# The first loads of a fused attention and feed-forward kernel: alpha and k of chunk 0 ahead of the first weight slice

## The chip, the cores and the metric

The kernel runs on one core of one Trainium2 chip. The metric is device time in microseconds (us), lower is better. The kernel before takes 539.71 us (median of three runs, 539.61 to 539.85).

## The reference

A gated recurrence over 768 tokens is computed for 4 batches and 8 heads of width 48. Its output, turned to 3072 rows of 384, goes through a feed-forward block with a hard-swish:

```python
for t in range(S):
    state = alpha[:, :, t, :, None] * state + einsum('bhd,bhe->bhde', k[:, :, t], v[:, :, t])
    y[:, :, t] = einsum('bhd,bhde->bhe', q[:, :, t], state)
x = y.transpose(0, 2, 1, 3).reshape(B * S, H * D)      # 3072 x 384
h = x @ w_in                                           # 384 x 2048
g = h * clip(h + 3, 0, 6) / 6
out = g @ w_out                                        # 2048 x 384
```

q, k, v and alpha are float32. w_in and w_out are float64; the chip gets their bits as pairs of 32-bit words.

## The kernel before

**Attention by chunks.** The tokens are cut into 24 chunks of 128 (six to a batch). Products of alpha over time are made with scans along the free axis, so alpha, k and q of a chunk are turned on TensorE first. For the first six chunks these inputs are loaded straight, 192 KB each and in pieces of 192 bytes, into a ring of three places.

**Weights by slices.** The two weight matrices arrive in 16 slices of 768 KB. Each float64 is decoded to a float32 by integer and float steps on ACT, DVE and GpSimd (POOL). Raw slices share five buffers, so later slices wait for the decoding of earlier ones.

**Feed-forward by groups.** Two chunks make a group of 256 tokens. The first groups use plain products; from group 1 or 2 on the two matrix products use sums of blocks, so that fewer block products are needed.

**The order.** There is no scheduler: one long list of words, read once from left to right, emits every instruction. Each word is a step with its chunk, slice or group and at times a PSUM bank. Each engine, and the Sync queue (SP) which issues all loads and stores, runs its own instructions in exactly that order; semaphores join the engines. Moving a word changes its place only in the queues that its instructions go to.

The words that the change and the prediction use:

| word | what it does | engine, lines |
|---|---|---|
| z.m.n | n idle 128x128 products of the identity into bank m, read by nobody | TensorE, L532, two instructions each |
| la.j, lk.j, lq.j | load alpha, k, q of chunk j | SP, L251 |
| lv.j | load v of chunk j in two halves | SP, L272 |
| w.i | load weight slice i | SP, L162 (w_in), L166 (w_out) |
| ta.j, tk.j, tq.j | turn alpha, k, q of chunk j | TensorE, L282 |
| ca.j | copy the turned alpha out of PSUM | ACT, L300 |
| r.j | scan of alpha from the chunk's end, and a reciprocal | DVE, L309, L313 |
| k.j, q.j | scale k by r.j, and q by p.j | DVE, L332 |
| p.j | scan of alpha from the chunk's start | DVE, L320 |
| d2.i | magnitude of slice i's high words (an activation with Abs) | ACT, L196 |
| d1.i | slice i's low words rounded (an activation with Copy) | ACT, L186 |
| dx.i | slice i's signs | ACT, L191 |
| d3.i | clamp and shift of slice i's high words | DVE, L203 and L205, or L207, L208 and L210 |
| d4.i | high and low words added | POOL, L217 |
| kb.j, ck.j | k.j turned back to rows by token, and copied out of PSUM | TensorE L374, ACT L378 |
| u.j | update of the state from k and v, two halves | TensorE, L429 |
| sm.j.b | new state after half b of chunk j | DVE, L437 (chunk 0, half 0), L439 |
| sv.j.b | state placed beside v (for chunk 0, half 0: zeros) | ACT, L419 (POOL, L415) |
| sc.j, m.j | scores within a chunk, and their mask | TensorE L346, DVE L356 |

qa.0.0 emits nothing, since chunk 0 starts a batch. The activations of d2 and d1 are `nc.scalar.activation(...)`; the copies of ca and ck are `nc.scalar.copy(...)`, which the profile shows as COPY and not as ACTIVATE. In program order the first instruction of ACT is d2.0, ahead of ca.0.

At the head of the list the Sync queue holds w.0, la.0, lk.0, la.1, lq.0, lk.1, lv.0 (two halves), la.2, w.2 and so on. TensorE holds 17 idle products, ta.0, tk.0, two idle products, ta.1, tq.0, kb.0, two idle products, u.0.

Of the kernel before, what the change touches and what calls it, by code (L numbers as in the profile page):

```python
# [17 lines left out]
def kernel(  # L18
# [553 lines left out]
    for i in range(8):  # L572
        r, o = divmod(i, 3)
# [175 lines left out]
    def run(words):  # L749
        for word in words.split():  # L750
            name, *at = word.split(".")
            steps[name](*(int(x) for x in at))

    with tc.manual_schedule():
        run("""z.0.5 z.0.3 z.0.1 z.0.8 qa.0.0 w.0 d2.0 d3.0 la.0 ta.0.0 ca.0 r.0 lk.0 tk.0.1 k.0
               z.0.2 p.0 la.1 ta.1.2 lq.0 tq.0.3 ca.1 r.1 lk.1 lv.0.0 sv.0.0 d1.0 kb.0.0 ck.0 z.0.2
               u.0.2.1 sm.0.0 sv.0.1 q.0 qa.0.1 tk.1.0 k.1 p.1 z.0.2 sc.0.2.3 m.0 la.2 ta.2.0 ca.2
               dx.0 w.2 d2.2 kb.1.0 ck.1 lq.1 r.2 sm.0.1 st.1 tq.1.2 q.1 d3.2 z.0.3 d1.2 dx.2
               lv.1.1 u.1.3.1 sv.1.0 sm.1.0 p.2 sm.1.1 sc.1.0.2 m.1 ya.0.3 yb.0 cy.0 lq.2 w.1 d1.1
# [179 lines left out]
```

## Time and profile before

| | |
|---|---|
| runs | 539.71, 539.85, 539.61 us |
| profiled execution: span from first to last instruction | 538.1 us |
| between the span and the median of the runs | 1.6 us |
| busy share of the span: TensorE, DVE, ACT, POOL | 98%, 88%, 48%, 9% |
| DMA: moved in the span, mean rate | 54.40 MB, 101 GB/s |
| granted TensorE clock | 1.000 |

The profile gives the span of the profiled execution; what lies around it is taken as the difference to the median of the runs, 1.6 us. In the views times are microseconds from the span's start. A row in order of time has start, duration, engine, line, operation, what is written and read with shapes and count, and in brackets the engine's idle time just before with what ended it. A row of waits has who waited, for whom, the total, how often, and the longest. The DMA view gives, for an issue, the time from issue to landing.

### The profile page before, as it was taken

How to read it: one execution, taken by the hardware profiler on the slowest of the kernel's cores; microseconds unless marked ns; L12 is line 12 of the kernel's file. 1: busy time of each engine (PE TensorE's matmuls, PEld its weight loads, DVE VectorE, ACT ScalarE, POOL GpSimd, SP SyncE). 2: the span in 40 equal slices, each digit the busy share in tenths (PEclk: the TensorE clock that was granted, in tenths of full speed). 3: DMA queues.
4: the chain of work that ended last, by engine and by line, in shares of the span. 5: the costliest groups of instructions: out<-in, count | busy, mean ns of one | idle time of the engine just before them, and what ended most of it. 6: DMA issues, size and time to landing. Idle time of an engine off the chain costs nothing.

```text
span 538.1 us, 15166 instructions
## 1 busy us (share of the span) xinstructions
PE 526.3 (98%) x6306; PEld 499.7 (93%) x6306; DVE 475.3 (88%) x839; ACT 259.6 (48%) x513; POOL 50.4 (9%) x71
## 2 busy tenths in 40 slices
PE   8799999999999999999999999999999999999997
PEld 7688886789999999999999999999999999999996
DVE  6999989999999899989999898999999898495481
ACT  3889865212653553543544444642644544553230
POOL 5333425100000000000010000000000000000000
PEclk9999999999999999999999999999999999999999
DMA  9998876006625156263444355155354042100001
GB/s 172 211 251 250 218 217 154 17 2 154 149 35 117 30 117 141 46 140 86 94 109 112 89 121 137 21 127 120 88 136 103 15 103 42 44 3 1 15 16 37
DMA packets 124101, 54.40 MB, mean 101 GB/s; under 512 B 83329, under 2 KB 116865, under 8 KB 124033
## 3 DMA queue, kind: packets, MB, share of 16 engines
q1 hardware_dynamic: 124032, 53.44, 43.7%
q8 instruction: 49, 0.80, 0.7%
q14 instruction: 20, 0.16, 0.1%
HBM read 44.50 MB, written 8.91 MB: 99 GB/s over the span
## 4 chain that ended last, share of the span: by engine, by line
PE 83%; DVE 10%; DMA 3%; ACT 1%; issue 1%; SPq 0%; POOL 0%; DVEq 0%; ACTq 0%; POOLq 0%
PE m_ps L703 32%; PE m_ps L600 32%; PE m_ps L478 6%; PE t_ps L455 4%; PE t_ps L346 2%; PE t_ps L429 2%; DMA v<-in_v_dram 2%; PE m_ps L532 1%; PE m_ps L489 1%; PE m_ps L516 1%; DVE rings L647 1%; DVE R L309 1%; DVE raw L537 1%; DVE g_sb L647 1%; DVE w L537 1%
## 5 line engine op out<-in xcount | busy, mean ns | idle before, releaser
L703 PE MATMUL m_ps<-w,g_sb 128*128 128x192 f32 x704 | 122.1, 327 | 0.6 <-ACT m_ps L709 0.5
L606 ACT COPY g_sb<-m_ps 128x512 f32<-128x512 f32 x110 | 63.5, 584 | 114.7 <-PE m_ps L600 98.2
L703 PEld LDWEIGHTS m_ps<-w,g_sb 128*128 128x128 f32 x704 | 113.7, 190 | 1.7 <-ACT m_ps L709 0.8
L703 PE MATMUL m_ps<-rings,g_sb 128*128 128x192 f32 x528 | 91.6, 327 | 0.6 <-ACT u L682 0.6
L703 PEld LDWEIGHTS m_ps<-rings,g_sb 128*128 128x128 f32 x528 | 85.3, 190 | 1.0 <-ACT u L682 0.9
L600 PE MATMUL m_ps<-xc,w 128*128 128x128 f32 x640 | 82.7, 277 | 0.2 <-DVE w L541 0.2
L600 PEld LDWEIGHTS m_ps<-xc,w 128*128 128x128 f32 x640 | 77.5, 192 | 1.4 <-issue 0.4
L494 ACT ACTIVATE r<-g_sb,half 128x512 f32<-128x512 f32 x80 | 56.7, 722 | 29.4 <-DVE g_sb L541 11.7
L498 DVE SCALAR_TENSOR_TENSOR g_sb<-r,g_sb 128x512 f32<-128x512 f32 x80 | 53.6, 682 | 7.5 <-ACT r L494 7.0
L600 PE MATMUL m_ps<-xT,raw 128*128 128x128 f32 x400 | 52.6, 278 | 0.9 <-ACT g_sb L606 0.9
L600 PEld LDWEIGHTS m_ps<-xT,raw 128*128 128x128 f32 x400 | 48.6, 192 | 1.9 <-ACT g_sb L606 1.2
L409 POOL TENSOR_TENSOR st<-sm,R 128x192 f32<-128x192 f32 x20 | 12.9, 643 | 355.8 <-DVE sm L439 306.7
L647 DVE TENSOR_TENSOR g_sb<-g_sb 128x512 f32<-128x512 f32 (+1 forms) x55 | 42.0, 792 | 1.4 <-PE m_ps L703 1.1
L600 PE MATMUL m_ps<-xT,w 128*128 128x128 f32 x320 | 42.0, 276 | 0.0
L600 PEld LDWEIGHTS m_ps<-xT,w 128*128 128x128 f32 x320 | 39.3, 192 | 0.1
L366 ACT COPY A<-q 48x256 f32<-48x256 f32 x88 | 35.6, 404 | 4.9 <-DVE q L332 3.7
L356 DVE TENSOR_TENSOR A<-t_ps,mask 64x256 f32<-64x256 f32 x96 | 36.1, 414 | 0.4
L478 PE MATMUL m_ps<-xT,w 128*128 128x256 f32 x144 | 32.8, 382 | 0.0
L600 PE MATMUL m_ps<-xc,raw 128*128 128x128 f32 x240 | 31.8, 276 | 0.0
L309 DVE TENSOR_TENSOR_SCAN R<-t,ones 128x516 f32<-128x516 f32 x24 | 29.5, 1231 | 1.3 <-ACT t L300 1.2
L478 PEld LDWEIGHTS m_ps<-xT,w 128*128 128x128 f32 x144 | 26.7, 190 | 3.6
L600 PEld LDWEIGHTS m_ps<-xc,raw 128*128 128x128 f32 x240 | 29.6, 192 | 0.1
(105 smaller groups left out, 730.0 us busy)
## 6 DMA issues: line engine op xcount, KB each, us to landing
raw<-in_moe_w_out_dram SPq DMA_DIRECT2D x8, 768.0 KB, 4.8
raw<-in_moe_w_in_dram SPq DMA_DIRECT2D x6, 768.0 KB, 7.0
v<-in_v_dram SPq DMA_DIRECT2D x48, 96.0 KB, 3.2
out_dram<-oh SPq DMA_DIRECT2D x44, 96.0 KB, 1.8
far<-kq SPq DMA_DIRECT2D x64, 64.0 KB, 2.2
kb<-far SPq DMA_DIRECT2D x64, 64.0 KB, 2.0
aq<-in_alpha_dram SPq DMA_DIRECT2D x36, 96.0 KB, 2.6
qq<-in_q_dram SPq DMA_DIRECT2D x36, 96.0 KB, 2.5
```

The costliest lines, as they stand in the source:

```text
L309: nc.vector.tensor_tensor_scan(out=reverse(R, n - 1, n), data0=reverse(ax, n, n), data1=reverse(ones, n, n), initial=0.0, op0=ALU.mult, op ...
L356: nc.vector.tensor_tensor(out=to[:, a], in0=sc[a][half], in1=mask[half, half].unsqueeze(1).to_broadcast([HB, NP, HB]), op=ALU.mult)
L366: nc.scalar.copy(out=to[:, a], in_=Q_t[j][64 * a : 64 * a + D, :, half])
L409: nc.gpsimd.tensor_tensor(out=st, in0=sm, in1=R_t[j][:, :, 0:1].to_broadcast([C, NP, D]), op=ALU.mult)
L455: nc.tensor.matmul(y_of(j, (i + 1) // 2, p)[:, HB * b : HB * b + HB], vb[:, p, e : e + 32], A_t[j][:, b, 2 * p + a], start=(b == 0 and i = ...
L478: nc.tensor.matmul(h[:, f], w1[:, kk, o : o + C], xT_t[g][:, kk], start=(kk == 0), stop=(kk == KT - 1))
L494: nc.scalar.activation(out=to, in_=h, func=AF.Relu, bias=half, scale=1.0 / 6.0)
L498: nc.vector.scalar_tensor_tensor(out=to, in0=r, scalar=1.0, in1=h, op0=ALU.min, op1=ALU.mult)
L600: nc.tensor.matmul(acc[g][i][:, f * C : (f + 1) * C], spots[w][:, f * C : (f + 1) * C], x_of(g, x), start=(first and f == 0), stop=last, s ...
L606: nc.scalar.copy(out=slots[z], in_=acc[g][i])
L647: nc.vector.tensor_tensor(out=out, in0=in0, in1=in1, op=ALU.subtract)
L703: nc.tensor.matmul(to[g], a, rhs[:, f], start=(first and f == 0), stop=(last and f == HF - 1), skip_group_check=True)
```

## The change

The head of the list is reordered. The words from w.0 to lk.0 and the decoding steps d2.0 and d3.0 change places, and the idle products at the start change in number.

```diff
-        run("""z.0.5 z.0.3 z.0.1 z.0.8 qa.0.0 w.0 d2.0 d3.0 la.0 ta.0.0 ca.0 r.0 lk.0 tk.0.1 k.0
-               z.0.2 p.0 la.1 ta.1.2 lq.0 tq.0.3 ca.1 r.1 lk.1 lv.0.0 sv.0.0 d1.0 kb.0.0 ck.0 z.0.2
+        run("""z.0.5 z.0.3 qa.0.0 la.0 lk.0 w.0 la.1 ta.0.0 ca.0 r.0 tk.0.1 k.0 z.0.6
+               p.0 ta.1.2 lq.0 ca.1 r.1 d2.0 tq.0.3 lk.1 lv.0.0 sv.0.0 d3.0 d1.0 kb.0.0 ck.0 z.0.2
                u.0.2.1 sm.0.0 sv.0.1 q.0 qa.0.1 tk.1.0 k.1 p.1 z.0.2 sc.0.2.3 m.0 la.2 ta.2.0 ca.2
```

Read by queue:

- SP: w.0, la.0, lk.0, la.1 becomes la.0, lk.0, w.0, la.1. All later loads keep their places.
- ACT: d2.0, ca.0, ca.1, d1.0, ck.0 becomes ca.0, ca.1, d2.0, d1.0, ck.0.
- DVE: d3.0, r.0, k.0, p.0, r.1, sm.0.0 becomes r.0, k.0, p.0, r.1, d3.0, sm.0.0.
- TensorE: the 17 idle products ahead of ta.0 become 8, and the two between tk.0 and ta.1 become six. The turns, kb.0 and u.0 keep their order.
- POOL: no step moves.

No instruction's shape, tile or bank changes, and nothing else in the list moves.

## The prediction

> **What bounds the kernel now.** I read the page first, for where the time sits.
>
> ```profile
> PE 526.3 (98%) x6306; PEld 499.7 (93%) x6306; DVE 475.3 (88%) x839; ACT 259.6 (48%) x513; POOL 50.4 (9%) x71
> PE 83%; DVE 10%; DMA 3%; ACT 1%; issue 1%; SPq 0%; POOL 0%; DVEq 0%; ACTq 0%; POOLq 0%
> ```
>
> The first row is busy time, the second the chain that ended last. TensorE fills the span, but that is an average over stages, and the edit touches only the first 14 us. So I asked next what DVE, the engine behind TensorE, waits for from 9.5 to 129 us.
>
> ```profile
> DVE s L439 <- PE t_ps L429: 1.3, 1, 1.3
> DVE R L309 <- ACT t L300: 1.2, 1, 1.2
> DVE w L207 <- ACT w L196: 0.5, 1, 0.5
> DVE k L332 <- PE t_ps L282: 0.2, 1, 0.2
> ```
>
> In 119.5 us DVE waits once for its first scan (r.0, L309, which starts at 9.46) and then 2.0 us in all. The opening quarter is thus a DVE queue without holes. ACT is nearly as full from 16 to 35 us. What delays the head of this queue delays all behind it, unless it disappears in those 2.0 us; what advances it helps only as far as its inputs arrive earlier too. So the third view is the head itself, DVE and then ACT in order of time:
>
> ```profile
> 9.46 1.24 DVE L309 TENSOR_TENSOR_SCAN R<-t,ones 128x516 f32<-128x516 f32 x1 [1.18 <-ACT t L300]
> 12.55 1.21 DVE L309 TENSOR_TENSOR_SCAN R<-t,ones 128x516 f32<-128x516 f32 x1
> 13.88 0.33 DVE L437 COPY s<-t_ps 128x192 f32<-128x192 f32 x1
> ```
>
> ```profile
> 0.74 1.28 ACT L196 ACT_TABLE_LOAD   x1 [0.74 <-PEq L921]
> 5.68 0.91 ACT L196 ACTIVATE w<-raw 128x768 f32<-128x768 f32 x1 [3.65 <-DMA raw<-in_moe_w_in_dram]
> 8.84 0.59 ACT L300 COPY t<-t_ps 128x512 f32<-128x512 f32 x1 [2.26 <-PE t_ps L282]
> 10.16 0.59 ACT L300 COPY t<-t_ps 128x512 f32<-128x512 f32 x1 [0.73 <-PE t_ps L282]
> 10.65 0.91 ACT L186 ACTIVATE raw<-raw 128x768 int32<-128x768 uint32 x1
> 12.30 0.59 ACT L378 COPY kb<-t_ps 128x512 f32<-128x512 f32 x1 [0.75 <-PE t_ps L374]
> ```
>
> sm.0.0 (L437, 13.88) is the first DVE step that needs the state update u.0 (L429 on TensorE, 12.99 to 13.77). u.0 needs ck.0 (L378, ends at 12.89) and the second half of lv.0, issued at 8.71 and landed 4.3 us later, at 13.0. Both arrive within 0.1 us of each other, so sm.0.0 is the point to follow. ACT's first row matters too: the table load carries the line of d2.0 (L196) and cost nothing, because ACT had 3.65 us to wait for the slice.
>
> **Part by part.** *Sync queue.* It issues one after another from 0.75 to 41 us. SP sees only the loads: w.0, la.0, lk.0, la.1 become la.0, lk.0, w.0, la.1, and all later loads keep their places. From issue start plus time to landing: w.0 5.7, la.0 6.8, lk.0 8.1, la.1 9.2, so a 192 KB load adds 1.2 us and a slice elsewhere 2.2 (w.2, 16.1 after la.2's 13.9) to 2.8 (w.1, 22.9 after lq.2's 20.1). w.0 took 4.9, so 2.1 to 2.7 of it is the start. The new order gives la.0 about 4.4, lk.0 5.6, w.0 8.1 and la.1 9.2 again. Bounds for la.1: 96 KB of v on an emptied queue landed in 2.7 us, with 0.6 more for 192 KB la.0 lands at 4.1, and the cheap slice gives 8.6; a start of 2.7 and the dear slice give 9.8. I take 9.2, in the middle, and hence no shift of any later load.
>
> *TensorE.* Ahead of ta.0 stand 8 idle products and not 17 (two instructions each):
>
> ```profile
> 1.46 6.91 PE L532 MATMUL m_ps<-ident 128*128 128x128 f32 x34 [1.46 <-POOL ident masks.py:199]
> ```
>
> 34 take 6.91, so 16 end near 4.9, just after la.0. ta.0, ca.0 and r.0 run about 3.6 us earlier (r.0 near 5.8). tk.0 comes at lk.0, 5.6; the six products behind it end by 8.9 at the starting pace, so ta.1 starts at the landing of la.1, 9.25, not behind products at 9.53: 0.28 gained.
>
> *DVE.* d3.0 (L203 0.92, L205 0.71) leaves the empty time before 9.46 and stands behind r.0, k.0, p.0 and r.1. Those need 4.3 us, and start 3.6 us sooner; r.1 waits for ca.1 and ends near 11.8. d3.0 costs nothing here, if it ends before sm.0.0 can start; without that cover it would cost its 1.6.
>
> *ACT.* d2.0 (L196, 0.91) moves from 5.68, where it was hidden, to behind ca.0 and ca.1; queued behind it are d1.0 and ck.0, and u.0 waits for ck.0. Before the edit d2.0 is the first ACT step. Behind it ACT's first steps are two copies, which are of another kind (COPY, not ACTIVATE). If the load stays with the first ACTIVATE, it too moves to behind ca.1, a step that waits for la.1. Its price is the row, 1.28; at the least it is 0 (it stays at the head), at the most I allow it twice.
>
> *The sum.* ta.1 from 9.25 (0.60, hand-over 0.03), ca.1 9.88 to 10.47, table load to 11.75, d2.0 to 12.66, d1.0 (0.1 overlapped) to 13.5, ck.0 to 14.0. Before, sm.0.0 came 0.99 after ck.0's end; now 15.0, against 13.88: **+1.1**. d3.0 runs from 12.7 to 14.3 and is covered. Of the 2.0 us of DVE waits, 1.5 end on TensorE and the remaining 0.5 on ACT, which the same delay moves, so I let nothing be absorbed. POOL has only d4.0, which waited behind d4.2 until 24.8, and loses nothing of its own. The span of 538.1 becomes 539.2; the 1.6 us between it and the median, 539.71, I leave as they are: 540.8.
>
> The Trainium skill, "ScalarE: Activation LUTs", section "What ACT_TABLE_LOAD costs", counts about 1.38 us of drain beside 1.28 for the load; by it the sum would be +2.5 and the time 542.2. This trace has 1.28 for the load, and any drain would be hidden in ACT's 3.65 us wait.
>
> **The rivals.** 0.2% is 1.08 us, about what a measurement of this kernel can tell from no change: under 538.63 is faster, over 540.79 slower.
>
> A, the forecast: the load sits on the path. With la.1 between 8.6 and 9.8 the delay is +0.5 to +1.7; less up to 0.2 for the wait at k.3, 540.0 to 541.4, about six in ten of it over the line. For it: the row's line number.
>
> B, no change: the load stays at ACT's head, since a COPY may want it as well; the trace has no COPY ahead of it. Then ca.1 ends at 10.47, d2.0 and d1.0 end by 12.2, ck.0 by 12.7, u.0 waits for lv.0 as before. 0 to -0.6 (by la.1's early bound): 539.1 to 539.7.
>
> C, faster: as B, and the loads gain over a microsecond. Narrow loads flow at a fixed number of packets (5198 in 6 us), while w.0 leaves most of its first 1.5 us empty (66 packets from 1.5 to 3.0). If alpha and k fill that time, the stream up to lv.0 shortens by up to 1.4, and DVE, ready 2.2 us sooner (3.6 less d3.0's 1.4 with its overlap), follows it. It decides from lv.0 landing before 11.9. Against it: from 18.0 to 19.5 the queue moved only 360 packets, with a slice queued behind narrow loads, so the empty stretch may only change place. 538.3.
>
> D, slower by more: TensorE stays slow.
>
> ```profile
> 2.00:4.00 2.00, 2.00 (x12) 2.00 (x11) 1.00 0.79 248
> 7.50:8.10 0.60, 0.60 (x8) 0.60 (x7) 1.00 1.51 163
> ```
>
> These are the idle products alone in two stretches (length, PE and PEld busy with counts, granted clock, DMA): one each 0.21 us up to 7.4, one each 0.11 after, at the same granted clock. The pace doubles after 5.9 us without a gap. The new order has possible gaps before ta.0 and tk.0, and one of 0.4 before ta.1. If the doubling is missed, ta.1 (+0.4), u.0 (up to +0.78) and sc.0 (up to +0.69) lengthen the path: +0.4 to +1.9 over A, 541.2 to 542.7, middle 541.9. The Trainium skill, "TensorE: Matmul & The Clock Gate", Part 1, says that a free-running window of 3.4 us must be busy; the trace agrees in so far as the doubling came 5.9 us after the first product.
>
> E, slower by more: ACT must empty around the load and it costs twice its row: +2.4, 542.1. That is the drain named above.
>
> **How the numbers follow.** A 0.50 (0.30 slower, 0.20 same), B 0.14 (same), C 0.16 (faster), D 0.15 and E 0.05 (slower). Slower 0.50, same 0.34, faster 0.16. The time is A's, 540.8; A's own range is 540.0 to 541.4. The 8-in-10 range runs from 538.9, which takes in B and leaves out most of C, to 542.0, which leaves out D's upper part and E.
>
> **What would show it.** ACT: the table load between the second COPY of L300 and L196, at about 10.5, with L378 ending near 14.0. DVE: L309 first near 5.8, L203 near 12.7, L437 near 15.0. SP: la.1 landing near 9.2, lv.0 near 13.0. TensorE: 0.11 between idle products before 8.9. The forecast is wrong if the table load stays at 0.74, if lv.0 lands a microsecond early, or if DVE takes the delay back before 129 us.

## The result

The changed kernel takes 538.56 us (median of 21 runs, 538.01 to 539.31) against 539.27 us for the kernel before (21 runs of the same comparison, 538.82 to 540.30). The ratio is 0.9987, 95% interval 0.9981 to 0.9993: 0.7 us or 0.13% faster, where 1.1 us slower was forecast. Timed again on another chip it gave 538.36 against 539.21, ratio 0.9987 (0.9979 to 0.9996). The gain is real and small; it stays inside the 0.2% that the prediction called no change.

The page of the profiled execution (span 537.4 us), busy time and the chain that ended last:

```profile
PE 524.8 (98%) x6296; PEld 498.2 (93%) x6296; DVE 475.1 (88%) x839; ACT 259.4 (48%) x513; POOL 50.2 (9%) x71
PE 80%; DVE 10%; ACT 4%; DMA 2%; issue 1%; SPq 1%; DVEq 0%; ACTq 0%
```

Ten TensorE instructions fewer, DVE and ACT as before. ACT in order of time shows at once what the forecast had wrong:

```profile
1.95 1.28 ACT L300 ACT_TABLE_LOAD   x1 [1.95 <-DVE t L108]
5.35 0.59 ACT L300 COPY t<-t_ps 128x512 f32<-128x512 f32 x1 [2.11 <-PE t_ps L282]
9.92 0.59 ACT L300 COPY t<-t_ps 128x512 f32<-128x512 f32 x1 [3.99 <-PE t_ps L282]
10.40 0.94 ACT L196 ACTIVATE w<-raw 128x768 f32<-128x768 f32 x1
11.22 0.91 ACT L186 ACTIVATE raw<-raw 128x768 int32<-128x768 uint32 x1
12.02 0.59 ACT L378 COPY kb<-t_ps 128x512 f32<-128x512 f32 x1
```

The table load now carries the line of ca.0 (L300). It precedes ACT's first copy, ends at 3.23 and is hidden again, because that copy waits for TensorE until 5.35. d2.0 (L196) follows ca.1 without a gap, and ck.0 (L378) ends at 12.61, where before it ended at 12.89. Then who DVE waits for between 5.5 and 129 us:

```profile
DVE R L309 <- ACT t L300: 3.2, 2, 1.8
DVE s L439 <- PE t_ps L429: 1.3, 1, 1.3
DVE s L437 <- PE t_ps L429: 0.6, 1, 0.6
```

From sm.0.0 (L437) on, DVE waits once, 1.3 us. The other two waits of the first trace of before, 0.2 (L332) and 0.5 (L207), are gone.

### The profile page after: what moved, and what is told of

It is laid out like the page before. It is cut to its first block, busy times and chain, and to the rows that moved or that the text cites. A ratio compares the mean times of both kernels' runs of the same rounds, so it can differ in the third digit from the quotient of the medians.

```text
span 537.4 us, 15147 instructions
## 1 busy us (share of the span) xinstructions
PE 524.8 (98%) x6296; PEld 498.2 (93%) x6296; DVE 475.1 (88%) x839; ACT 259.4 (48%) x513; POOL 50.2 (9%) x71
## 4 chain that ended last, share of the span: by engine, by line
PE 80%; DVE 10%; ACT 4%; DMA 2%; issue 1%; SPq 1%; DVEq 0%; ACTq 0%
PE m_ps L703 33%; PE m_ps L600 32%; PE m_ps L478 5%; PE t_ps L455 4%; PE t_ps L429 2%; PE t_ps L346 2%; DMA rings<-in_q_dram 1%; PE m_ps L489 1%; DVE g_sb L498 1%; ACT raw L191 1%; DVE rings L647 1%; PE t_ps L282 1%; DVE raw L537 1%; DMA kq<-in_k_dram 1%; DVE g_sb L647 1%
## 5 line engine op out<-in xcount | busy, mean ns | idle before, releaser
L409 POOL TENSOR_TENSOR st<-sm,R 128x192 f32<-128x192 f32 x20 | 12.9, 644 | 356.3 <-DVE sm L439 307.1
```

The costliest lines, as they stand in the source:

```text
L409: nc.gpsimd.tensor_tensor(out=st, in0=sm, in1=R_t[j][:, :, 0:1].to_broadcast([C, NP, D]), op=ALU.mult)
```

## Which trace to believe

The two profiled spans differ by 0.6 us, nearly as much as the medians, and an easy story offers itself: in the changed kernel lv.2 landed at 32.2 and not at 34.3, TensorE's 0.53 us wait for it at 34.35 vanished, and DVE's two later waits with it. Two kernels tested that story, the kernel before profiled again, and the kernel before with lv.2 moved up.

> The kernel before, unchanged, profiled a second time. Two theories of the 0.7 us that the change gained. Theory S (the stream): the new order of the first three loads brings the later loads forward, and lv.2, which TensorE waits for, lands 2.1 us sooner (32.2 against 34.3 in the two traces); then this second profile of the kernel before shows lv.2's second half at 34.3 within 0.5, and DVE's wait of 0.2 to 0.5 at L332 near 38.8. Theory N (scatter): later loads land a microsecond or two earlier or later in every execution whatever their order, and the 0.7 us comes from something else; then lv.2 lands here anywhere from 32 to 35.

Measured: span 537.5, and lv.2 landed at 32.4. DVE's waits from 9 to 129 us:

```profile
DVE s L439 <- PE t_ps L429: 1.3, 1, 1.3
DVE R L309 <- ACT t L300: 1.0, 1, 1.0
DVE s L437 <- PE t_ps L429: 0.3, 1, 0.3
```

The unchanged kernel has none of those waits here. The landing at 34.3 was scatter of one execution.

```diff
-  ... fa.1.2 lq.3 ck.2 d1.3 p.3 d3.3 lv.2.2 u.2.3.2
+  ... fa.1.2 lv.2.2 lq.3 ck.2 d1.3 p.3 d3.3 u.2.3.2
```

> The kernel before with one word moved: lv.2 is issued ahead of lq.3 and not behind it. Nothing else changes. Theory S, in the part that TensorE's wait for lv.2 (0.53 us at 34.35) and DVE's two waits behind it (0.2 and 0.5) are what the change removed: lv.2 lands 1.2 us sooner, at 33.1, and the kernel gains 0.4 to 0.7 against before. Theory N: within 0.2 of the kernel before.

Measured: 539.13 against 539.21, ratio 0.9997 (0.9989 to 1.0006), and lv.2 landed at 31.5. Nothing is gained; the story falls. What holds sm.0.0 in the second trace of the unchanged kernel is visible in DVE's order of time (some rows), and in u.0's row on TensorE:

```profile
12.40 1.21 DVE L309 TENSOR_TENSOR_SCAN R<-t,ones 128x516 f32<-128x516 f32 x1
13.64 0.18 DVE L313 RECIPROCAL t<-R 128x4 f32<-128x4 f32 x1
14.15 0.36 DVE L437 COPY s<-t_ps 128x192 f32<-128x192 f32 x1 [0.33 <-PE t_ps L429]
15.03 0.68 DVE L332 TENSOR_TENSOR k<-t_ps,R 128x512 f32<-128x512 f32 x1
```

```profile
13.44 0.68 PE L429 MATMUL t_ps<-v,kb 64*64 64x48 f32 x30 [0.29 <-DMA v<-in_v_dram]
```

DVE is ready at 13.8 and waits 0.33 us for u.0 (L429), and u.0 for the second half of lv.0. That half's issue and its time to landing, here and in the third trace of the changed kernel (the row joins both halves; the second is issued at 8.84 and at 8.03, and so lands at 13.4 and at 12.3):

```profile
7.63 1.83 SPq L272 DMA_DIRECT2D v<-in_v_dram  x2
v<-in_v_dram SPq DMA_DIRECT2D x1, 96.0 KB, 4.6
```

```profile
7.13 1.53 SPq L272 DMA_DIRECT2D v<-in_v_dram  x2
v<-in_v_dram SPq DMA_DIRECT2D x1, 96.0 KB, 4.2
```

In all five traces with the old order of loads (two of the kernel before, three of other kernels) it landed at 13.0, 13.4, 13.3, 13.2 and 12.9 (mean 13.2). With the new order it landed at 12.7, 12.9 and 12.3 in three traces of the changed kernel, and at 12.6, 12.7, 12.8 and 13.0 in four other kernels (mean of the seven 12.7). That is what the texts below call theory H: lv.0 lands about 0.5 us earlier, the engines ahead of u.0 are ready for it, and DVE's queue carries the gain on. The ranges touch, at 12.9 to 13.0, so a single trace would not show it. lv.0 is not alone in this place: la.1 landed earlier too, so ck.0 ended at 12.09 to 12.60 in the changed kernel against 12.74 and 12.89 before, each time less than 0.4 us ahead of lv.0 there.

## The changed kernel twice more

> The changed kernel, unchanged, profiled once more, to see it with the clock granted in full: of its 21 runs 15 had a mean granted clock of 0.999 or 1.000 (median 538.4) and six had 0.996 or 0.997 (median 539.1), and the profiled one was of the six. Theory H (head): lv.0 lands 0.5 us earlier than in the traces of the kernel before (12.7 against 13.0 to 13.4), and at full clock u.0 ends and sm.0.0 (L437) starts near 13.5 against 13.9 to 14.15; the queue of DVE carries that to the end, span 536.6. Rival F (fewer idle products, no head): sm.0.0 starts at 13.9 or later as in the first trace and the span is 536.6 all the same. If the clock drops here too: L437 near 13.9 and a span of 537.3.

Measured: 538.85 us, span 537.1, clock in full. lv.0 landed at 12.9 and sm.0.0 starts at 13.66: earlier than in the second trace of the kernel before, against rival F, but later than the 13.5 of theory H, and the span is 0.5 longer than expected.

> The changed kernel once more, to stand on the same chip as the three kernels beside it. Theory H (lv.0 lands 0.4 us earlier and the head of ACT and DVE is ready for it, and DVE's queue carries that to 129 us): 0.3 to 0.7 below the kernel before. Rival (nothing gained that holds on another chip): within 0.2.

Measured: 538.36 against 539.21, as told above. Its profiled execution has a span of 536.4, with lv.0 landed at 12.3. DVE in order of time (q.0, between the last two rows, is left out):

```profile
10.02 1.23 DVE L309 TENSOR_TENSOR_SCAN R<-t,ones 128x516 f32<-128x516 f32 x1
11.29 0.18 DVE L313 RECIPROCAL t<-R 128x4 f32<-128x4 f32 x1
11.38 0.66 DVE L203 TENSOR_SCALAR w<-w 128x768 f32<-128x768 f32 x1
12.08 0.69 DVE L205 TENSOR_SCALAR w<-w 128x768 uint32<-128x768 uint32 x1
13.02 0.36 DVE L437 COPY s<-t_ps 128x192 f32<-128x192 f32 x1 [0.25 <-PE t_ps L429]
13.89 0.68 DVE L332 TENSOR_TENSOR k<-t_ps,R 128x512 f32<-128x512 f32 x1
```

d3.0 (L203, L205) fits between r.1 and sm.0.0 and delays nothing; sm.0.0 starts at 13.02, 1.1 earlier than in the second trace of the kernel before. That DVE's queue carries such a shift to the end can be read by setting the start of k.1 (the third row of L332) beside the span:

| trace | sm.0.0 | k.1 | span | span less k.1 |
|---|---|---|---|---|
| before, second | 14.15 | 15.03 | 537.45 | 522.42 |
| before, lv.2 moved up | 14.03 | 14.90 | 537.41 | 522.51 |
| changed, first | 13.90 | 14.92 | 537.45 | 522.53 |
| changed, second | 13.66 | 14.53 | 537.05 | 522.52 |
| changed, third | 13.02 | 13.89 | 536.43 | 522.54 |
| loads alone | 14.23 | 15.07 | 537.51 | 522.44 |
| changed, old idle products | 15.12 | 15.97 | 538.40 | 522.43 |
| changed, 13 idle products | 13.78 | 14.65 | 537.15 | 522.50 |

Over 2.1 us of k.1 the rest of the span stays at 522.4 to 522.5. These eight are the traces in which DVE has only its one wait of 1.3 us between k.1 and 129 us. In the six others it has 0.4 to 0.9 us of further waits there, and the rest of the span is 523.1 to 523.5, or 524.5 with the second table load.

## One part at a time

The half-speed stretches told below scatter the runs, and some of these kernels have them in most of theirs, so for each kernel the median of all runs and that of the runs at full granted clock (mean 0.999 or 1.000) are given. In these comparisons the kernel before has 539.21 to 539.41 over all runs and 539.03 to 539.16 at full clock; the changed kernel has 538.36 (15 runs) and 538.29 (10 runs).

**Loads alone.**

```diff
-  ... z.0.1 z.0.8 qa.0.0 w.0 d2.0 d3.0 la.0 ta.0.0 ca.0 r.0 lk.0 tk.0.1 k.0 ...
+  ... z.0.1 z.0.8 qa.0.0 la.0 lk.0 w.0 d2.0 d3.0 ta.0.0 ca.0 r.0 tk.0.1 k.0 ...
```

> Only the loads are reordered (la.0, lk.0, w.0, la.1); d2.0 and d3.0 stay ahead of ca.0 and r.0, and the idle products stay. w.0 should land near 8, so d2.0 runs 8.0 to 8.9, ca.0 to 9.5, r.0 from 9.5 unless d3.0 (two steps, 1.4 us from 8.9) comes first: r.0 at about 10.3, and sm.0.0 at about 14.7 against 13.9. Theory S expects the gain of the later loads with a head that is 0.8 late: -0.7 to +0.2 against the kernel before, and lv.2 landing before 33. Theory N expects +0.6 to +0.9.

Measured: 541.07 against 539.21, ratio 1.0029 (1.0018 to 1.0040); at full clock 539.29 against 539.16 (three runs of twelve). Most of the 1.9 us thus comes with the half-speed stretches, which nine runs had; even the fastest run, 539.12, is only level with the kernel before. lv.0 landed at 12.6, earlier as in the changed kernel, but DVE could not use it:

```profile
8.49 0.69 DVE L203 TENSOR_SCALAR w<-w 128x768 f32<-128x768 f32 x1 [4.31 <-ACT w L196]
9.83 1.22 DVE L309 TENSOR_TENSOR_SCAN R<-t,ones 128x516 f32<-128x516 f32 x1
14.23 0.33 DVE L437 COPY s<-t_ps 128x192 f32<-128x192 f32 x1
```

d3.0 waits for the later slice, r.0 stands behind it, and from 8.49 to sm.0.0 DVE has no gap. lv.2 landed at 31.6 here, before 33 as theory S had it, and still nothing was gained.

**Steps alone.**

```diff
-  ... w.0 d2.0 d3.0 la.0 ... ca.1 r.1 lk.1 lv.0.0 sv.0.0 d1.0 ...
+  ... w.0 la.0 ... ca.1 r.1 d2.0 lk.1 lv.0.0 sv.0.0 d3.0 d1.0 ...
```

> Only the compute steps are moved: d2.0 behind ca.1 and d3.0 behind r.1, as in the change; the loads keep the old order and the idle products their old number. Theory H: lv.0 still lands at 13.0 to 13.4, so sm.0.0 stays at 13.9 to 14.15 and the time is that of the kernel before, within 0.2 us, in runs of equal clock. Rival (the moved decoding itself gains, since ACT and DVE no longer decode ahead of chunk 0): -0.4 to -0.8.

Measured: 540.09 against 539.41, ratio 1.0013 (1.0004 to 1.0022); at full clock 539.75 against 539.12 (four runs, 539.12 to 540.23). Worse than theory H said. r.0 starts at 8.80, because 17 idle products still stand ahead of ta.0, and with d3.0 in the same queue DVE runs without a gap until sm.0.0 at 14.53, behind lv.0's 13.2. I had looked at lv.0 only and left out that DVE's own queue becomes the bound.

**Idle products alone**, and **the change without them.**

> The kernel before with the changed kernel's idle products alone: 8 ahead of ta.0 in place of 17, six behind tk.0 in place of two. Theory H: la.0 lands at 6.9, so ta.0 comes 1.3 us sooner, but r.0 still stands behind d3.0 (8.3) and sm.0.0 behind lv.0 (13.2): no gain, within 0.2 at full clock, and more runs with a half-speed window than the kernel before. Rival (the fewer idle products are the gain): -0.4 to -0.7.

Measured: 539.91 against 539.21, ratio 1.0012 (1.0003 to 1.0021); at full clock 539.49 against 539.03 (four runs of eleven). In the profiled execution idle products still ran at the starting pace, one instruction each 0.21 us, at 11 us, against 7.4 in the first trace, and sm.0.0 started at 15.21. Fewer idle products alone are no gain; in this execution TensorE stayed slow for longer.

> The changed kernel with the old idle products (17 and two). Theory H: r.0 waits for ta.0 at 8.2, so it starts near 9.4, and with d3.0 behind r.1 in the same queue sm.0.0 comes near 15.0 in place of 13.7: 0.8 to 1.3 above the changed kernel, 0.3 to 0.8 above the kernel before. Rival (idle products cost nothing but their own empty time): the same as the changed kernel.

Measured: 540.22 against 539.21, ratio 1.0014 (1.0005 to 1.0023); at full clock 539.13 (four runs, 538.82 to 539.75), 0.8 over the changed kernel, and 0.1 over the kernel before where 0.3 to 0.8 was expected. The steps come as expected:

```profile
9.39 1.23 DVE L309 TENSOR_TENSOR_SCAN R<-t,ones 128x516 f32<-128x516 f32 x1 [5.21 <-ACT t L300]
15.12 0.34 DVE L437 COPY s<-t_ps 128x192 f32<-128x192 f32 x1
```

So none of the three parts gains alone, nor do the first two together without the third. sm.0.0 needs both lv.0, which only the new loads bring forward, and DVE's queue, which takes 5.7 us from r.0 to sm.0.0 with d3.0 in it. To reach the 13.02 to 13.90 of the changed kernel, r.0 must therefore start by 7.3 to 8.2; there it started at 5.97 to 6.75, here at 9.39.

## What the forecast's table load would have cost

The changed kernel with an explicit second table load in the place where the forecast had put the first.

```diff
-  ... ca.1 r.1 d2.0 tq.0.3
+  ... ca.1 r.1 pl d2.0 tq.0.3      # pl: nc.scalar.preload_act_table(AF.Abs)
```

> The changed kernel with a second activation table load placed between ca.1 and d2.0, where the forecast had put the first one. This prices the step of the forecast that did not happen. If the load costs its 1.28 us there and DVE has no slack behind it, as the forecast had it: +1.1 over the changed kernel, +0.4 against the kernel before, with L378 ending near 14.0 and sm.0.0 at 15.0. If a drain of about as much comes with it: +2.5 and +1.8. If later stages take it back: under +0.3 over the changed kernel.

Measured: 540.56 against 539.21, ratio 1.0023 (1.0015 to 1.0032). Two of its eleven runs had the full clock, 539.42 and 539.56: 1.1 to 1.2 over the changed kernel, as the sum had it, though on two runs only. Nine runs had half-speed stretches and 540.3 to 541.6. ACT:

```profile
9.48 0.58 ACT L300 COPY t<-t_ps 128x512 f32<-128x512 f32 x1 [2.75 <-PE t_ps L282]
10.08 1.28 ACT L746 ACT_TABLE_LOAD   x1
11.37 0.89 ACT L196 ACTIVATE w<-raw 128x768 f32<-128x768 f32 x1
12.96 0.56 ACT L378 COPY kb<-t_ps 128x512 f32<-128x512 f32 x1
```

The load starts 0.02 us after the copy, takes 1.28, and d2.0 follows after 0.01. There is no gap on either side, so rival E's price is refuted for a second load for a function already in use (Abs, as d2); the 1.38 us that the Trainium skill ("ScalarE: Activation LUTs", section "What ACT_TABLE_LOAD costs") adds for a switch does not appear here. A switch between two different sets was not tried. The trace does not repeat the sum step by step: ca.1 came 0.4 earlier than forecast, so L378 ended at 13.52 and not 14.0, and sm.0.0 started at 14.34 and not 15.0; a half-speed stretch follows, so its span of 539.8 cannot be set beside the sum.

## The half-speed stretch

In the changed kernel's first trace TensorE is empty from 7.59 to 9.26. Three stretches, all engines (length, busy time and count of PE, PEld, DVE, ACT and POOL, granted clock, DMA):

```profile
7.60:9.20 1.60, 0.00 (x0) 0.00 (x0) 1.53 (x2) 0.00 (x0) 0.00 (x0) 1.00 1.19 163
11.20:14.50 3.30, 3.16 (x43) 2.80 (x42) 2.62 (x6) 1.55 (x4) 0.00 (x0) 0.50 1.03 257
14.60:18.00 3.40, 2.52 (x46) 1.86 (x44) 3.33 (x7) 2.73 (x6) 0.00 (x0) 1.00 1.05 183
```

For one stretch of 3.4 us the granted clock is 0.50. TensorE in the changed kernel's first and third trace, u.0 (L429):

```profile
12.70 1.16 PE L429 MATMUL t_ps<-v,kb 64*64 64x48 f32 x32
```

```profile
12.19 0.79 PE L429 MATMUL t_ps<-v,kb 64*64 64x48 f32 x32 [0.72 <-ACT kb L378]
```

1.16 us at half speed, 0.79 at full. One such stretch lowers the mean granted clock by 3.4 x 0.5 / 537 = 0.003, and that is how runs can be told apart: six of the changed kernel's 21 runs show 0.996 or 0.997 and have a median of 539.06, the other 15 have 538.36. So a slow TensorE, which rival D feared, does come, in some runs only, and those runs are 0.7 us longer. It is not D's own mechanism: D had the doubling at the start missed, but here the pace had doubled by 4.4 us. D's own mechanism shows in the trace of the idle products alone, where TensorE was still at the starting pace at 11 us.

> The changed kernel with 13 idle products between tk.0 and ta.1 in place of six, to fill TensorE's empty 1.67 us (7.6 to 9.26). Theory H with the clock as the reason for its two groups of runs: no run at 0.997, all at 0.999 or 1.000, and the median 538.4, that is 0.15 to 0.3 below the changed kernel's. Rival: the drop comes from later gaps and stays in a third of the runs; or ta.1 gets behind the idle products and loses 0.2.

Measured: 539.14 against 539.41, ratio 0.9994 (0.9985 to 1.0003); two of eleven runs still at 0.997, and 539.01 at full clock. The products did not remove the stretch and did not gain over the changed kernel; its profiled lv.0 landed at 13.0, late for the new order, and I cannot say how much of the time that explains.

What sets the stretch off was not tested by a run of its own, but the traces narrow it down. Five of them have such a stretch in the head. Each is 3.41 us long and begins 6.8, 10.2 or 17.1 us after the opening pace doubled, that is two, three or five times 3.41, so the clock seems to be set anew in slots of that length. What TensorE did in the slot just before:

| trace | pace doubles at | half-speed stretch | TensorE busy in the 3.41 us before |
|---|---|---|---|
| changed, first | 4.34 | 11.16 to 14.58 | 1.35 |
| second table load | 7.62 | 14.45 to 17.86 | 1.32 |
| changed, old idle products | 7.32 | 17.56 to 20.97 | 1.77 |
| steps alone | 6.09 | 23.15 to 26.57 | 1.69 |
| idle products alone | 13.13 | 23.37 to 26.79 | 1.68 |

Twelve traces record when the pace doubled. If each is cut into such slots, no other slot of the first 45 us has TensorE busy for less than 1.92 us. So a slot that is empty for about half of its length or more was followed by a half-speed slot, and no fuller one was. Where the slots fall depends on when the pace doubled, which would explain why the same gap costs in some runs only. This is read from five stretches and stays a reading. Over all runs the mean clock was below 0.999 in 18 of 89 of the kernel before, in none of 11 with lv.2 moved, in 9 of 12 of the loads alone, in 9 of 11 with the second table load, and in 7 of 11 each of the steps alone, the idle products alone and the old idle products.

## Two versions that go further

The wait for la.1 is used for decoding, kb.0 and ck.0 come ahead of ta.1, lv.0 is loaded ahead of lk.1, and six idle products are added.

```diff
-  ... k.0 z.0.6 p.0 ta.1.2 lq.0 ca.1 r.1 d2.0 tq.0.3 lk.1 lv.0.0 sv.0.0 d3.0 d1.0 kb.0.0 ck.0 z.0.2 ...
+  ... k.0 z.0.7 p.0 kb.0.0 d2.0 ck.0 d3.0 z.0.4 ta.1.2 lq.0 ca.1 r.1 tq.0.3 lv.0.0 sv.0.0 lk.1 d1.0 z.0.3 ...
```

> The changed kernel with what theory H says still holds sm.0.0: lv.0 is loaded ahead of lk.1 (so it lands 1.2 us sooner, near 11.5), d2.0 and d3.0 fill the time in which ACT and DVE wait for la.1, kb.0 and ck.0 come ahead of ta.1, and idle products fill TensorE's gap. sm.0.0 should start at about 12.4 against 13.5; k.1 then waits for lk.1 until 13.4 against 14.5, and the later loads (lq.1, lv.1) allow about 0.8 to 1.2 of that: 537.3 to 537.8. If the queue of DVE is not what carries the head to the end: 538.4, as the changed kernel at full clock.

Measured: 538.37 against 539.41, ratio 0.9983 (0.9974 to 0.9992), span 536.5. sm.0.0 started at 12.17, as expected; the time is above the 537.3 to 537.8 expected and is the 538.4 that stood for DVE's queue not carrying the head to the end. In its trace k.1 starts 0.9 before the changed kernel's third, and DVE waits 0.4 us more at L332 and 0.5 at L207 further on.

```diff
-  ... d3.0 z.0.4 ta.1.2 ...
+  ... d3.0 z.0.1 ta.1.2 ...
```

> The earlier reordering (lv.0 ahead of lk.1; d2.0, d3.0, kb.0 and ck.0 in the wait for la.1) with one idle product ahead of ta.1 in place of four, so that ca.1 and r.1 come 0.6 us sooner. In the trace of that reordering sm.0.0 already started at 12.2, DVE then waited 0.2 at 24, 0.2 at 37 and 0.5 at 64.6, and TensorE had no gap from 23.3 to 64. Theory T (from 23 us on TensorE is the bound once the head is 1.5 us early): no further gain, 0.6 to 0.9 below the kernel before and up to 0.3 below the changed one. Rival (DVE's queue still carries all of it): 1.2 to 1.5 below the kernel before.

Measured: 538.18 against 539.21, ratio 0.9989 (0.9979 to 0.9999); at full clock 538.15 against the changed kernel's 538.29 and the 539.03 of the kernel before, as theory T had it. DVE's waits from 5.5 to 129 us say where the rest went:

```profile
DVE R L309 <- ACT t L300: 1.8, 1, 1.8
DVE s L439 <- PE t_ps L429: 1.3, 1, 1.3
DVE w L207 <- ACT w L196: 0.4, 1, 0.4
DVE k L332 <- PE t_ps L282: 0.2, 1, 0.2
```

sm.0.0 is at 11.83, 1.2 before the changed kernel's third trace, and the span, 536.3, is 0.2 shorter. DVE gives back 0.2 at L332 (36.8 us), behind TensorE, which is busy 31.00 of the 31 us from 33 to 64, and 0.45 at L207 (64.3 us). In this trace the head thus no longer decides from there on. Both versions beat the kernel before; neither is shown to beat the changed one, as the intervals overlap.

## Why the prediction was wrong, point by point

The forecast of 540.8 was 2.2 us too long: 1.1 for the table load, 0.7 for a gain that was put at nothing, and 0.4 because the base was taken too high.

- *ACT.* The step that failed. I let the line number of the table load decide that it belongs to the first ACTIVATE, and put it behind ca.1, on the path of u.0. In every trace it stands ahead of ACT's first instruction, COPY or not, as rival B had it; in the changed kernel it ran from 1.95 to 3.23 while ACT waited, and cost nothing. Without it the forecast's own sum ends at no change. Its price, 1.28 for the row and +1.1 in all, agrees with the two runs at full clock of the kernel that has a load in that place.
- *Sync queue.* The term "no shift of any later load" was mis-sized. la.0 landed 3.1 to 3.2 us after its issue, at 3.8 to 4.0 (4.4 forecast, 4.1 as the early bound), la.1 at 9.1 and 8.6 in the two traces that give its landing (9.2 taken, 8.6 as the early bound), and lv.0 about 0.5 us earlier than with the old order. Part of my error is that the one trace I had showed lv.0 at 13.0, the second earliest of five.
- *TensorE.* ta.1 started at 9.26, 9.20 and 8.74 (9.25 forecast). r.0 started at 5.97, 6.75 and 6.75, up to 0.9 later than the 5.8 forecast, because TensorE kept its starting pace for longer in two of the traces; r.0 was early enough all the same.
- *DVE.* d3.0 is covered, as said. The queue without holes and its one-to-one carrying are borne out over 2.1 us, in the eight traces without further waits.
- *The rivals.* B's mechanism happened, without its statement that u.0 waits for lv.0 as before; its range was 0 to -0.6 by la.1's early bound, and -0.7 was measured. C's 538.3 lies nearest to the measured 538.56, but by luck, since it was reckoned from the base of 539.71. Its condition, lv.0 before 11.9, was not met (12.3 to 12.9 in the three traces). Its mechanism was partly there: from 1.5 to 3.0 us 1145 packets moved in the changed kernel's first trace, against 66 before, and the stream up to lv.0 became about 0.5 shorter, not 1.4. D's slow TensorE came in another form, as told. E's drain did not appear.
- *The base.* 539.71 came from three runs; 21 gave 539.27. A forecast of "no change" would have had to carry that, too: 538.56 is below the line of 538.63 drawn for "faster" only because the line was drawn from 539.71.

## What to carry to other kernels

When a step is moved behind others of its engine, look at what the program puts in front of it by itself, such as a table load, and find out which instruction it is tied to before charging it to the path. If an early queue has no holes, as DVE's here, its head can be priced from two arrivals, the last load and the queue's own sum, and a reordering gains only where both come sooner and no later wait takes the gain back. Before explaining a difference between two traces, profile the old kernel once more: the largest difference here, 2.1 us in one landing, was scatter.

## What the runs showed of the hardware

TensorE started at half pace in every trace, one idle product each 0.42 us at 4 us (two instructions of 0.21), and the doubling came at different times for the same work: at 7.5 and 6.3 us in two kernels whose head is the same (the kernel before, and that with lv.2 moved), at 4.3, 6.3 and 6.6 in the three traces of the changed kernel, and at 13.1 in that of the idle products alone. The granted clock is 1.00 in the rows of that opening stretch, and 0.50 in the later one, so the mean clock tells of the second only. And a 192 KB load in pieces of 192 bytes landed 3.1 to 3.2 us after issue on an empty queue, where a 768 KB slice took 4.9; the same load behind that slice took 5.6.
